# Linear attention and a gated MLP on one core: loads and transposes as a stream of their own, weight fold and norms re-paced, scheduler constants changed

## The chip, the cores and the metric

The kernel runs on one core of a Trainium2 chip. The metric is device time in microseconds (us) of one execution. Repeated executions of one kernel here mostly lie within 0.5% of each other (the six of the kernel before: 284.86 to 285.74 us; the widest fast set of a changed kernel, e11: 284.05 to 286.36); one execution of one experiment, e6, fell into a much slower state (487.29 us at a granted clock of 0.559) and is set aside below. The engines are PE (matrix multiply), DVE (vector), ACT (scalar, with the exponentials), POOL (general purpose) and SP, whose queue issues all DMA transfers of this kernel, one after the other (79 in the trace of the kernel before, no two issues overlapping).

## The reference

One input `x` of 2048 tokens by 640 is normalised, then goes through a linear attention with 32 heads of 20 and through a gated MLP of width 1536. The sum of both and of `x` is the result.

```python
def _A_ref(x, wqkv, w_phi, wo):
    qkv = (x @ wqkv).reshape(B, S, 3, H, Dh) ...            # q, k, v: [1, 32, 2048, 20]
    pq = einsum("bhsd,hdf->bhsf", q, w_phi);  pk = einsum("bhsd,hdf->bhsf", k, w_phi)
    phi_q = concatenate([softmax(pq), softmax(-pq)], -1)    # phi_k the same from pk
    kv = einsum("bhsf,bhsd->bhfd", phi_k, v);  z = einsum("bhsf->bhf", phi_k)
    o = einsum("bhqf,bhfd->bhqd", phi_q, kv) / (einsum("bhqf,bhf->bhq", phi_q, z)[..., None] + 1e-6)
    return o... @ wo
def _B_ref(x, w1, w3, w2):
    return (silu(x @ w1) * (x @ w3)) @ w2
xn = layernorm(x)
return x + _A_ref(xn, ...) + _B_ref(xn, ...)
```

## The kernel before

Tokens are handled in 16 tiles of 128. For each tile: load `x`, layer norm (statistics on DVE, the power on POOL, the application on DVE or ACT), transpose to `xnT` (tiles 0 to 3 on PE, tiles 4 to 15 by a transposing DMA), then keys (`Wkp`) and values (`wv`). `Wkp` is the key weight with `w_phi` folded in; this "fold" is 30 small matmuls that need the transposed `wk` (in `wqkT`) and a block diagonal `BDc` that POOL builds from `w_phi` (`phi_s`). MLP groups (10 matmuls of 512 columns each) do not depend on the attention and serve as filler.

The order of instructions on each engine is fixed when the program is built, by a list scheduler in Python. Each part of the work is a generator, a "stream". The scheduler keeps estimated times, takes the stream whose next piece can start first, and appends it. In the traces PE keeps to that order, waiting on semaphores: the ten matmuls that e9's list has before the keys of tile 4 instead of after those of tile 5 start at 30.67 us in the kernel before, and in e9 they run in the stretch from 22.76 to 26.86, before those keys. So an estimate that is too hopeful costs a real stall: in the hole of 2.0 us shown below, PE stands still although matmuls that could run come later in its list.

```python
    def commit(self, ops):                      # the scheduler's model of a DMA
        ...
            if o.dma:
                self.free[o.eng] = t + 0.45
                if "T" == o.part:
                    self.free[o.eng] = t + max(2.6, o.cost / 150e3)
                self.bus = max(self.bus, t + 0.4) + o.cost / 340e3
                o.end = self.bus + 1.6
...
    def loads():
        x(0, 1); x(1, 2); x(2, 4)                               # [cut: written out]
        P.dma("SP", wv[:], wqkv_t[:, :, 2 * D:3 * D])
        P.dma("SP", phi_s[:], phi_t)
        P.dma("SP", wqkT[:, DC:2 * DC, :], A_wqkv[:, D:2 * D], True)   # transposing
        x(4, 8)
        w13(0, 512)
        x(8, 12)
        w13(512, 1024)
        x(12, 16)
...
    def attention():
        ...
        yield v(2)
        for dc in range(DC):
            yield lambda dc=dc: fold_mm(1, dc, banks(2))
        yield v(3)
        for t in range(T):
            yield lambda t=t: k_tile(t, banks(2))
            done["k"] = t + 1
            if 2 <= t < 14:
                yield from transposed(t + 2)
            if t == 3:
                yield lambda: w13(1024, 1536)
            if t == 5:
                yield lambda: P.dma("SP", wqkT[:, 0:DC, :], A_wqkv[:, 0:D], True)
            if t >= 4:
                yield v(t)
        ...
    streams = [norms(), attention(), k_norms(), o_transposes(), mlps(), outs()]
```

The softmax here doesn't subtract the row's maximum and nothing guards it: scores larger than these inputs give would overflow.

Of the kernel before, what the change touches and what calls it, by code (L numbers as in the profile page):

```python
# [9 lines left out]
D = 640  # L10
# [3 lines left out]
T = S // 128  # L14
DC = D // 128
# [27 lines left out]
class _Program:  # L43
# [3 lines left out]
    def __init__(self, nc):  # L47
        self.nc = nc
        self.eng = {"PE": nc.tensor, "ACT": nc.scalar, "DVE": nc.vector,
                    "POOL": nc.gpsimd, "SP": nc.sync}  # L50
        self.base = {}
        self.ops = []
        self.free = dict.fromkeys(ENGINES, 0.0)
        self.bus = 0.0
        self.last_w = {}
        self.last_r = {}
        self.bank = {}
        self.pending = None
        self.pool = None
# [107 lines left out]
    def commit(self, ops):  # L167
        for o in ops:
            o.idx = len(self.ops)
            o.deps = self.find_deps(o)  # L170
            t = self.free[o.eng]
            for d in o.deps:
                t = max(t, d.end + 0.07)
            o.start = t
            if o.dma:
                self.free[o.eng] = t + 0.45
                if "T" == o.part:
                    self.free[o.eng] = t + max(2.6, o.cost / 150e3)
                self.bus = max(self.bus, t + 0.4) + o.cost / 340e3
                o.end = self.bus + 1.6  # L180
            else:
                o.end = t + o.cost
                self.free[o.eng] = o.end
            self.ops.append(o)
            if o.eng == "POOL" and not o.dma:
                self.pool = o
            for g in o.reads:
                if isinstance(g, tuple):
                    self.bank.setdefault(g, {})[o.eng] = o
                else:  # L190
                    self.last_r.setdefault(g, {})[("dma", o.idx) if o.dma else o.eng] = o
            for g in o.writes:
                if isinstance(g, tuple):
                    self.bank.setdefault(g, {})[o.eng] = o
                else:
                    self.last_w[g] = o
                    self.last_r.pop(g, None)
# [45 lines left out]
def bass_parallel_sum__linear_kernel_hedgehog__glu_gated_swiglu__prompt_kernel(  # L243
# [154 lines left out]
    def w13(a, b):  # L398
        P.dma("SP", w1_s[:, :, a:b], w1_t[:, :, a:b])
        P.dma("SP", w3_s[:, :, a:b], w3_t[:, :, a:b])  # L400

    def loads():
        def x(a, b):
            P.dma("SP", x_tok[:, a:b, :], x_t[:, a:b, :])

        x(0, 1)
        x(1, 2)
        x(2, 4)
        P.dma("SP", wv[:], wqkv_t[:, :, 2 * D:3 * D])
        P.dma("SP", phi_s[:], phi_t)  # L410
        P.dma("SP", wqkT[:, DC:2 * DC, :], A_wqkv[:, D:2 * D], True)
        x(4, 8)
        w13(0, 512)
        x(8, 12)
        w13(512, 1024)
        x(12, 16)


    def consts():
# [45 lines left out]
    def xn_transpose(t, k):  # L465
        for dc in range(DC):
            tr(PSb[:, k * 1024 + 128 * dc:k * 1024 + 128 * dc + 128],
               x_tok[:, t, 128 * dc:128 * dc + 128])
        src = PSb[:, k * 1024:k * 1024 + D].rearrange("p (c n) -> p c n", n=128)
        evac(xnT[:, :, t * 128:(t + 1) * 128], src)  # L470
# [152 lines left out]
                       default=0.0)  # L623
        return min(range(0, 8, n), key=free_at)

    done = dict.fromkeys(("ln", "t", "k", "n", "kv", "q", "o", "h"), 0)

    def norms():
        yield lambda: (loads(), consts())
        for t in range(4):  # L630
            yield lambda t=t: ln_stats(t, 1)
            if t % 2:
                yield lambda t=t: ln_apply(t - 1)
                done["ln"] = t
                yield lambda t=t: ln_apply(t)
                done["ln"] = t + 1
        yield block_diag
        for t in range(4, T, 2):
            while t > done["t"] + 4:
                yield None  # L640
            yield lambda t=t: ln_stats(t, 2)
            if t > 4:
                yield lambda t=t: ln_apply(t - 2)
                yield lambda t=t: ln_apply(t - 1)
                done["ln"] = t
        yield lambda: ln_apply(T - 2)
        yield lambda: ln_apply(T - 1)
        done["ln"] = T
        yield consts_late

    def k_norms():
        for t in range(T):
# [5 lines left out]
    def transposed(t):  # L658
        while done["ln"] <= t:
            yield None  # L660
        if t < 4:
            yield lambda: xn_transpose(t, banks(1))
        else:
            yield lambda: P.dma("SP", xnT[:, :, t * 128:(t + 1) * 128], x_tok[:, t, :], True)
        done["t"] = t + 1

    def attention():
        def v(t):
            return lambda: v_tile(t, banks(2))

        yield lambda: warm_up(10, True)
        yield from transposed(0)
        yield lambda: warm_up(4, False)
        yield from transposed(1)
        yield v(0)
        yield v(1)
        yield from transposed(2)
        yield from transposed(3)
        yield v(2)
        for dc in range(DC):  # L680
            yield lambda dc=dc: fold_mm(1, dc, banks(2))
        yield v(3)
        for t in range(T):
            yield lambda t=t: k_tile(t, banks(2))
            done["k"] = t + 1
            if 2 <= t < 14:
                yield from transposed(t + 2)
            if t == 3:
                yield lambda: w13(1024, 1536)
            if t == 5:  # L690
                yield lambda: P.dma("SP", wqkT[:, 0:DC, :], A_wqkv[:, 0:D], True)
            if t >= 4:
                yield v(t)
            if 9 <= t < 14:
                yield lambda dc=t - 9: fold_mm(0, dc, banks(2))
        yield lambda: P.dma("SP", wo_s[:], A_wo.rearrange("(c p) d -> p c d", p=128))
        for fc in range(DC):
            yield lambda fc=fc: q_proj(0, fc, banks(1))
        while done["n"] < T:
            yield None  # L700
        for fc in range(DC):
            for sg in range(2):
                yield lambda fc=fc, sg=sg: kv_sum(sg, fc, banks(1))
        done["kv"] = 1
        yield lambda: P.dma("SP", w2_s[:], B_w2.rearrange("(c p) d -> p c d", p=128))
        yield lambda: (load_xres(0), load_xres(1))
        for b in range(NB):
            for j in range(4):
                t = 4 * b + j
                yield lambda t=t: q_tok(t, banks(4))  # L710
                done["q"] = t + 1
                if b + 1 < NB:
                    for fc in range((5 * j + 3) // 4, (5 * j + 8) // 4):
                        yield lambda b=b, fc=fc: q_proj(b + 1, fc, banks(1))
# [8 lines left out]
    def mlps():  # L723
        for b in range(NB):
            for fc in range(FC):
                while done["t"] < 4 * b + 4 or b == 2 and done["t"] < T or b == 3 and not done["kv"]:
                    yield None
                yield lambda b=b, fc=fc: mlp(b, fc, banks(2))
            done["h"] = b + 1
# [4 lines left out]
                yield None  # L734
            yield lambda t=t: out_tile(t, banks(2))

    streams = [norms(), attention(), k_norms(), o_transposes(), mlps(), outs()]
    n = len(streams)
    heads, alive = [None] * n, [True] * n
    while any(alive):  # L740
        best = None
        for i in range(n):
            if heads[i] is None and alive[i]:
                s = next(streams[i], StopIteration)
                if s is StopIteration:
                    alive[i] = False
                else:
                    heads[i] = s
            if heads[i] is None:
                continue  # L750
            save = nmlp[0], len(finish)
            ops = P.step(heads[i])
            after = nmlp[0], finish[save[1]:]
            nmlp[0] = save[0]
            del finish[save[1]:]
            if any(o.eng == "PE" for o in ops):
                at = max(P.ready(ops), P.free["PE"] + 0.15)
            else:
                at = P.start_of(ops[0])
                if i == 2:  # L760
                    at -= 4.0
                if i == 0 and at < P.free["PE"] + 2.0:
                    at = -1.0
            if best is None or at < best[0]:
                best = (at, i, ops, after)
        if best is None:
            continue
        at, i, ops, after = best
        nmlp[0] = after[0]
        finish.extend(after[1])  # L770
        P.commit(ops)
        heads[i] = None
# [61 lines left out]
```

## Time and profile before

| | before |
|---|---|
| median of 6 runs | 285.38 us (284.86 to 285.74) |
| span of the profiled run | 283.2 us, granted PE clock 1.000 |
| first useful matmul / end of the last | 6.01 / 280.7 us |

The page of the kernel before; in part 2 each digit is the busy share of one fortieth of the span, in tenths, and part 4 is the chain of waits that ended last:

```profile
span 283.2 us, 4601 instructions
PE 274.6 (97%) x1873; PEld 168.4 (59%) x1890; DVE 181.1 (64%) x317; ACT 107.8 (38%) x194; POOL 59.5 (21%) x90
PE   7897999999999999999999999999999999999996
PE 82%; DVE 6%; DMA 6%; SPq 3%; issue 2%; ACT 0%
```

A slice is 7.08 us. Only the first four slices and the last have visible room; the fourth, from 21.2 to 28.3 us, stands at 7. From the fifth on PE is the limit: busy 90% or more in each slice but the last, and 82% of the chain. Note that 1873 matmuls are recorded but 1890 weight loads: 17 matmul records are missing.

What PE waited for, kernel before (total us, times, longest):

```profile
PE PS L101 <- DMA xnT<-x_tok: 1.8, 1, 1.8
PE PS L101 <- DVE t_68 L101: 1.6, 2, 1.3
PE PS L101 <- DVE x_tok L101: 0.8, 2, 0.6
PE PS L101 <- ACT xnT L101: 0.5, 1, 0.5
```

The longest wait is for one transposed tile. The timeline of PE around it (start, duration, what, count; in brackets the idle time before it and who ended it):

```profile
16.99 5.60 PE L101 MATMUL PS<-Wkp,xnT 128*128 128x320 bf16 x40
22.64 2.10 PE L101 MATMUL PS<-xnT,w_s 128*128 128x512 bf16 x9
26.59 1.53 PE L101 MATMUL PS<-Wkp,xnT 128*128 128x320 bf16 x10 [1.84 <-DMA xnT<-x_tok]
```

Four tiles of keys, one MLP group (one record missing), then nothing until the keys of tile 4 at 26.59. The issues on the SP queue in that stretch, same columns:

```profile
11.62 3.13 SPq L113 DMA_DIRECT2D w_s<-in_B_w_dram  x2
14.79 1.79 SPq L113 DMA_DIRECT2D x_tok<-in_A_x_dram  x1
18.36 4.95 SPq L113 DMA_TRANSPOSE xnT<-x_tok  x2
```

And the same moment in the chain of waits, in order of time: the transpose issued at 18.36 landed 8.18 us later, at 26.54.

```profile
18.36 8.18 DMA xnT<-x_tok
26.54 0.05 issue
26.59 9.12 PE PS L101 x60
```

The three loads ahead of it (w1 and w3 columns 512 to 1024, x tiles 12 to 15, 1.9 MB) landed at 22.3, 24.2 and 26.0 (landing times that no line here shows are read from the landing records of the packed trace). Of the eight later transposes of the same form, issued from 49.05 us on with no load ahead, six landed in 2.6 us, the other two in 3.3 and 3.9.

### The profile page before, as it was taken

What the parts mean: (1) busy time and instruction counts of PE and PEld (TensorE: products, weight loads), DVE (VectorE), ACT (ScalarE), POOL (GpSimd) and SP (SyncE); (2) the same over time, 40 slices, a digit from 0 to 9 for tenths busy, and PEclk for the clock granted to TensorE, in tenths of its full rate; (3) what the DMA queues carried; (4) which work ended last, traced back from release to release, by engine and by line L of the source; (5) the groups of instructions that cost most, each with busy time, mean ns of one, the idle gap of its engine ahead of it and who ended that gap; (6) DMA issues with size and microseconds to landing.
All of it is one profiled execution on the core that took longest, in us unless ns stands there. A gap on an engine that the chain in (4) does not pass through costs nothing.

```text
span 283.2 us, 4601 instructions
## 1 busy us (share of the span) xinstructions
PE 274.6 (97%) x1873; PEld 168.4 (59%) x1890; DVE 181.1 (64%) x317; ACT 107.8 (38%) x194; POOL 59.5 (21%) x90
## 2 busy tenths in 40 slices
PE   7897999999999999999999999999999999999996
PEld 2664644666765965555555555544467777777774
DVE  4589986987772468998998999999731212121212
ACT  2596644697976035446446453332200000000000
POOL 4548970387586100000000000000000000000000
PEclk9999999999999999999999999999999999999999
DMA  7999900242500065411112111132002131312211
GB/s 215 282 352 264 262 1 1 49 46 56 155 0 2 0 203 146 44 29 23 25 23 45 27 24 23 29 44 46 0 2 93 49 93 46 95 54 85 70 51 46
DMA packets 39654, 21.96 MB, mean 78 GB/s; under 512 B 26704, under 2 KB 39632, under 8 KB 39632
## 3 DMA queue, kind: packets, MB, share of 16 engines
q1 hardware_dynamic: 39632, 21.66, 30.6%
q8 instruction: 15, 0.25, 0.4%
q14 instruction: 7, 0.06, 0.1%
HBM read 12.81 MB, written 2.62 MB: 54 GB/s over the span
## 4 chain that ended last, share of the span: by engine, by line
PE 82%; DVE 6%; DMA 6%; SPq 3%; issue 2%; ACT 0%
PE PS L101 82%; SPq L113 3%; DMA xnT<-x_tok 3%; DMA x_tok<-in_A_x_dram 3%; DVE prod L101 2%; DVE t_68 L101 1%; DVE den_s L101 1%; DVE hT_79 L101 1%; DVE g_s L101 0%; DVE hT_71 L101 0%; DVE pr_s L101 0%; DVE xres L101 0%; ACT e_s L101 0%; DVE o_tok L101 0%
## 5 line engine op out<-in xcount | busy, mean ns | idle before, releaser
L101 PE MATMUL PS<-xnT,w_s 128*128 128x512 bf16 x468 | 105.9, 379 | 1.0 <-DVE t_68 L101 0.3
L101 PEld LDWEIGHTS PS<-xnT,w_s 128*128 128x128 bf16 x480 | 46.6, 98 | 55.6 <-DVE prod L101 0.6
L101 DVE TENSOR_TENSOR xres<-PS,xres 128x640 bf16<-128x640 f32 (+2 forms) x17 | 13.4, 786 | 60.0 <-PE PS L101 60.0
L101 ACT ACTIVATE th<-PS 128x512 f32<-128x512 f32 x48 | 28.7, 598 | 53.5 <-PE PS L101 53.5
L101 DVE SCALAR_TENSOR_TENSOR t_68<-th,PS 128x512 bf16<-128x512 f32 x48 | 32.6, 680 | 14.2 <-ACT th L101 14.2
L101 POOL TENSOR_TENSOR ekt<-ekt,rS_62 128x640 bf16<-128x640 bf16 x32 | 39.7, 1270 | 7.3 <-DVE rS_62 L101 7.2
L101 DVE TENSOR_REDUCE S_61<-ekt 128x64 f32<-128x1280 bf16 x16 | 23.5, 1467 | 6.9 <-ACT ekt L101 6.9
L101 PE MATMUL PS<-Wkp,xnT 128*128 128x320 bf16 x160 | 23.9, 299 | 1.8 <-DMA xnT<-x_tok 1.8
L101 PE MATMUL PS<-wv,xnT 128*128 128x320 bf16 x160 | 24.2, 299 | 0.7 <-ACT xnT L101 0.5
L101 PE MATMUL PS<-wo_s,oT 128*128 128x320 bf16 (+2 forms) x160 | 24.5, 299 | 0.0
L101 DVE TENSOR_TENSOR prod<-PS,g_s 128x1280 bf16<-128x1280 f32 x16 | 23.9, 1491 | 0.5
L101 ACT ACTIVATE ekt<-PS 128x640 bf16<-128x640 f32 x32 | 20.6, 706 | 6.8 <-PE PS L101 6.7
L101 PE MATMUL PS<-xnT,Wqp 128*128 128x512 bf16 x95 | 22.6, 379 | 0.3
L101 PEld LDWEIGHTS PS<-Wkp,xnT 128*128 128x128 bf16 x160 | 15.4, 98 | 8.0 <-DMA xnT<-x_tok 2.3
L101 PEld LDWEIGHTS PS<-wv,xnT 128*128 128x128 bf16 x160 | 15.4, 98 | 7.6 <-ACT xnT L101 0.7
L101 PEld LDWEIGHTS PS<-wo_s,oT 128*128 128x128 bf16 x160 | 15.7, 98 | 6.3
L101 DVE BATCH_NORM_STATS2 bst<-x_tok 128x6 f32<-128x320 bf16 x32 | 15.2, 476 | 5.1 <-DMA x_tok<-in_A_x_dram 4.6
L101 PEld LDWEIGHTS PS<-xnT,Wqp 128*128 128x128 bf16 x100 | 9.4, 98 | 8.8
L101 ACT ACTIVATE v_82<-PS 128x640 bf16<-128x640 f32 x16 | 11.5, 716 | 8.3 <-PE PS L101 8.0
L101 ACT ACTIVATE e_s<-PS 128x64 f32<-128x64 f32 x32 | 9.0, 283 | 14.5 <-PE PS L101 13.5
L101 PE MATMUL PS<-w_s,hT_79 128*128 128x320 bf16 (+2 forms) x96 | 13.9, 299 | 0.0
L101 PE MATMUL PS<-w_s,hT_77 128*128 128x320 bf16 x96 | 13.7, 299 | 0.0
(57 smaller groups left out, 268.3 us busy)
## 6 DMA issues: line engine op xcount, KB each, us to landing
w_s<-in_B_w_dram SPq DMA_DIRECT2D x6, 640.0 KB, 7.1
xres<-in_A_x_dram SPq DMA_DIRECT2D x16, 160.0 KB, 2.4
out_dram<-xres SPq DMA_DIRECT2D x15, 160.0 KB, 1.8
x_tok<-in_A_x_dram SPq DMA_DIRECT2D x3, 640.0 KB, 8.4
w_s<-in_B_w_dram SPq DMA_DIRECT2D x1, 1920.0 KB, 8.4
wv<-in_A_wqkv_dram SPq DMA_DIRECT2D x1, 800.0 KB, 5.5
wo_s<-in_A_wo_dram SPq DMA_DIRECT2D x1, 800.0 KB, 4.9
x_tok<-in_A_x_dram SPq DMA_DIRECT2D x2, 160.0 KB, 2.4
```

Of the source, the lines that this page charges most:

```text
L101: o = _Op(eng, lambda: m(*args, **kw), r, w, cost)
L113: o = _Op(eng, lambda: m(out, in_), self.regions(in_), self.regions(out), nbytes, True)
```

## The change

The intent: issue the transposes from a stream of their own and put later weight loads behind them, so that the keys need not wait; fold `wk` whenever it lands; load `phi` and `wv` first, `x` tiles 2 and 3 after them; pace the norms by finished keys; and correct the constants of the scheduler's DMA model. No arithmetic changes. The core of the diff:

```diff
-        self.free = dict.fromkeys(ENGINES, 0.0)
+        self.free = dict.fromkeys(ENGINES, 0.8)
-                    self.free[o.eng] = t + max(2.6, o.cost / 150e3)
-                self.bus = max(self.bus, t + 0.4) + o.cost / 340e3
+                    self.free[o.eng] = t + max(1.3, o.cost / 150e3)
+                self.bus = max(self.bus, t + 0.5) + o.cost / (280e3 if o.part else 320e3)
...
-        x(2, 4)
+        P.dma("SP", phi_s[:], phi_t)
         P.dma("SP", wv[:], wqkv_t[:, :, 2 * D:3 * D])
-        P.dma("SP", phi_s[:], phi_t)
+        load_x(2, 4)
         P.dma("SP", wqkT[:, DC:2 * DC, :], A_wqkv[:, D:2 * D], True)
-        x(4, 8)
+        load_x(4, 8)
         w13(0, 512)
-        x(8, 12)
-        w13(512, 1024)
-        x(12, 16)
+        load_x(8, 12)
...                                             # norms(): block_diag after tile 1, and
-            while t > done["t"] + 4:
+            while t > done["k"] + 6:
                 yield None
...
+    def fold_k():                               # a stream; before: in line after v(2)
+        for dc in range(DC):
+            yield lambda dc=dc: fold_mm(1, dc, banks(2))
+        done["f"] += 1
...
+    def loads():                                # a stream; before: inside attention()
+        while done["t"] < 4: yield None
+        for t in range(4, T):
+            while done["ln"] <= t: yield None
+            yield lambda t=t: P.dma("SP", xnT[:, :, t * 128:(t + 1) * 128], x_tok[:, t, :], True)
+            done["t"] = t + 1
+            if t == 7:
+                yield lambda: (w13(512, 1024), load_x(12, 16))
+                done["w"] = 8
+            if t == 9:
+                yield lambda: w13(1024, 1536)
+                done["w"] = 12
+                yield lambda: P.dma("SP", wqkT[:, 0:DC, :], A_wqkv[:, 0:D], True)
+                done["f"] = 2
...
-    streams = [norms(), attention(), k_norms(), o_transposes(), mlps(), outs()]
+    streams = [norms(), attention(), k_norms(), loads(), fold_k(), o_transposes(), mlps(), outs()]
-                if i == 2:
+                if i == 2 and at < P.free["PE"] + 3.0:
                     at -= 4.0
```

More of the change, by code (lines that the diff above doesn't have):

```diff
@@ L400, in w13, with load_x, first_loads @@
         P.dma("SP", w3_s[:, :, a:b], w3_t[:, :, a:b])
-    def loads():
-        def x(a, b):
-            P.dma("SP", x_tok[:, a:b, :], x_t[:, a:b, :])
-        x(0, 1)
-        x(1, 2)
-        x(2, 4)
+    def load_x(a, b):
+        P.dma("SP", x_tok[:, a:b, :], x_t[:, a:b, :])
+    def first_loads():
+        load_x(0, 1)
+        load_x(1, 2)
+        P.dma("SP", phi_s[:], phi_t)
         P.dma("SP", wv[:], wqkv_t[:, :, 2 * D:3 * D])
-        P.dma("SP", phi_s[:], phi_t)
+        load_x(2, 4)
         P.dma("SP", wqkT[:, DC:2 * DC, :], A_wqkv[:, D:2 * D], True)
-        x(4, 8)
+        load_x(4, 8)
         w13(0, 512)
-        x(8, 12)
-        w13(512, 1024)
-        x(12, 16)
+        load_x(8, 12)
     def consts():
@@ L624, in banks @@
         return min(range(0, 8, n), key=free_at)
-    done = dict.fromkeys(("ln", "t", "k", "n", "kv", "q", "o", "h"), 0)
+    done = dict.fromkeys(("w", "ln", "t", "f", "k", "n", "kv", "q", "o", "h"), 0)
     def norms():
-        yield lambda: (loads(), consts())
+        yield lambda: (first_loads(), consts())
         for t in range(4):
@@ L636, in norms @@
                 done["ln"] = t + 1
-        yield block_diag
-        for t in range(4, T, 2):
-            while t > done["t"] + 4:
+            if t == 1:
+                yield block_diag
+        todo = []
+        for t in range(4, T + 2, 2):
+            if t == T or t > done["k"] + 6:
+                for u in todo:
+                    yield lambda u=u: ln_apply(u)
+                    done["ln"] = u + 1
+                todo = []
+            if t == T:
+                break
+            while t > done["k"] + 6:
                 yield None
             yield lambda t=t: ln_stats(t, 2)
-            if t > 4:
-                yield lambda t=t: ln_apply(t - 2)
-                yield lambda t=t: ln_apply(t - 1)
-                done["ln"] = t
-        yield lambda: ln_apply(T - 2)
-        yield lambda: ln_apply(T - 1)
-        done["ln"] = T
-        yield consts_late
+            for u in todo:
+                yield lambda u=u: ln_apply(u)
+                done["ln"] = u + 1
+            todo = [t, t + 1]
+        yield consts_late
+    def fold_k():
+        for dc in range(DC):
+            yield lambda dc=dc: fold_mm(1, dc, banks(2))
+        done["f"] += 1
+    done["w"] = 4
     def k_norms():
@@ L660, in transposed @@
             yield None
-        if t < 4:
-            yield lambda: xn_transpose(t, banks(1))
-        else:
-            yield lambda: P.dma("SP", xnT[:, :, t * 128:(t + 1) * 128], x_tok[:, t, :], True)
+        yield lambda: xn_transpose(t, banks(1))
         done["t"] = t + 1
+    def loads():
+        while done["t"] < 4:
+            yield None
+        for t in range(4, T):
+            while done["ln"] <= t:
+                yield None
+            yield lambda t=t: P.dma("SP", xnT[:, :, t * 128:(t + 1) * 128], x_tok[:, t, :], True)
[8 more added lines that the diff above has]
+                done["f"] = 2
     def attention():
@@ L679, in attention @@
         yield v(2)
-        for dc in range(DC):
-            yield lambda dc=dc: fold_mm(1, dc, banks(2))
         yield v(3)
+        while done["f"] < 1:
+            yield None
         for t in range(T):
+            while done["t"] <= t:
+                yield None
             yield lambda t=t: k_tile(t, banks(2))
             done["k"] = t + 1
-            if 2 <= t < 14:
-                yield from transposed(t + 2)
-            if t == 3:
-                yield lambda: w13(1024, 1536)
-            if t == 5:
-                yield lambda: P.dma("SP", wqkT[:, 0:DC, :], A_wqkv[:, 0:D], True)
             if t >= 4:
@@ L694, in attention @@
             if 9 <= t < 14:
+                while done["f"] < 2:
+                    yield None
                 yield lambda dc=t - 9: fold_mm(0, dc, banks(2))
@@ L725, in mlps @@
             for fc in range(FC):
-                while done["t"] < 4 * b + 4 or b == 2 and done["t"] < T or b == 3 and not done["kv"]:
+                while done["t"] < 4 * b + 4 or done["w"] <= fc or b == 2 and done["t"] < T or b == 3 and not done["kv"]:
                     yield None
```

## The prediction

> **What bounds the kernel now.** The matrix engine. The page gives PE 97% of a 283.2 us span, and the chain of waits is PE for 82%. The start-to-start pitch in the timeline is 0.216 us for a 512-column matmul, so PE streams back to back[...]. I count pitches, not busy shares. Summing pitches, useful matmuls need about 268 us (264.6 recorded, plus an estimated 3.7 for the roughly 17 records missing). What is left to win:
> - the start, to the first real matmul at 6.01 us, and four warm-up matmuls after it: kept;
> - small holes between 7.5 and 15.6 us: 1.8 us together (the wait views name the norms of tiles 2 and 3 and one xnT copy, 1.1 us);
> - one hole at 24.4 to 26.6 us, 2.0 us: PE <- DMA xnT<-x_tok;
> - about 0.9 us near 187 to 194 us, PE <- DVE (t);
> - the tail after the last matmul, 2.5 us.
> So about 5 us (1.8%) is there at all; over 2% would need more than the holes hold.
>
> **What the change does to them.**
> 1. The 2.0 us hole. The transpose of token tile 4 is issued at 18.36 and lands at 26.54, 8.2 us, because w1, w3 (512 to 1024) and x tiles 12 to 15 (1.9 MB, issued from 11.6 us, landing at 22.3, 24.2 and 26.0) sit ahead of it. Uncrowded transposes of the same form later (49.05 us) land in 2.6 us. The change issues those loads after tile 7's transpose, so tile 4 should land at about 21 to 21.5 us (estimate: 18.4 + 2.6 to 3), before PE finishes the keys of tile 3 at 22.3. The hole goes: -2.0 us.
> 2. The fold of wk can run when wk lands (10.9 us, before: 13.5) and fills PE's waits for tiles 2 and 3. But x tiles 2 and 3 now queue behind wv's 0.8 MB: they land at about 8 us, not 5.3, and their norms slip by about 1 us. Net -0.3 us (between -0.8 and +0.5).
> 3. The later weight loads land about 8 us later. First use of w1, w3 (512 to 1024) needs four MLP groups and several key tiles done first, over 15 us of PE work, so no wait.
> 4. Norms paced by keys move DVE and POOL work earlier, without changing its amount. DVE is 64% busy overall but 92% from 140 to 180 us; a differently mixed order can lose or win up to 1 us there. Expected 0.
> 5. The scheduler's new constants only change order; work and bytes stay the same.
>
> All of it is on the chain, since PE is continuous from 26.6 to 280.7 us: a hole removed early moves the end by as much, unless DVE gives it back after 170 us.
>
> **Prediction.** 285.4 - 2.0 - 0.3 = 283.1 us, range 281.2 to 285.3. Faster by over 2%: 0.03; within 2%: 0.95; slower: 0.02.
>
> **What would show it.** Right: the wait PE <- DMA xnT gone; tile 4's transpose landing about 3 us after issue; key tile 0 starting at 16.5 to 17.3 us; wk's fold before the second pair of transposes; recorded matmul counts and PE's total pitch unchanged. Wrong: PE waiting on w_s, on Wkp or on the x_tok norms of tiles 2 and 3; a larger PE <- DVE t wait after 170 us.
>
> **What would make it wrong.** PE in program order stalls where the scheduler's model is too hopeful: its transposes now cost 1.3 us of issue, the trace shows 1.2 to 3.2 in the crowded stretch. Several such stalls would eat the 2 us.

## The result, and the profile after

| | before | after |
|---|---|---|
| median of 6 runs | 285.38 us | 283.12 us (282.78 to 283.43) |
| ratio after / before | | 0.9921 (95%: 0.9908 to 0.9935) |
| span of the profiled run | 283.2 us | 281.4 us |

Executions over 1.5% slower than the fastest of the same kernel are left out of the means. A ratio is the mean time of one kernel's fast runs over that of the other's in the same rounds, so it is not quite the ratio of the medians quoted. All these runs are at clock 1.0. The gain of 0.8% is clear of noise.

The page of the kernel after:

```profile
span 281.4 us, 4619 instructions
PE 275.2 (98%) x1890; PEld 168.6 (60%) x1890; DVE 180.6 (64%) x317; ACT 108.6 (39%) x194; POOL 59.3 (21%) x90
PE   7799999999999999999999999999999999999996
PE 87%; DVE 6%; DMA 3%; issue 1%; SPq 1%; ACT 1%
```

The fourth slice of PE is now full; the second fell from 8 to 7. All 1890 matmuls are recorded here, so "PE busy" rose by 0.6 us for no reason of work: it is the missing records of before. PE's waits after:

```profile
PE PS L101 <- DVE t_68 L101: 1.6, 2, 1.3
PE PS L101 <- DMA wqkT<-in_A_wqkv_dram: 0.9, 1, 0.9
PE PS L101 <- DMA wv<-in_A_wqkv_dram: 0.5, 1, 0.5
PE PS L101 <- ACT Wkp L101: 0.5, 1, 0.5
```

The wait for the DMA of `xnT` is gone; three small new ones (1.9 us) stand where those for `x_tok` and the copy of `xnT` (1.3 us) stood. The timeline of PE shows both:

```profile
8.13 2.88 PE L101 MATMUL PS<-wv,xnT 128*128 128x320 bf16 x20 [0.49 <-DMA wv<-in_A_wqkv_dram]
11.89 0.47 PE L101 MATMUL PS<-BDc,wqkT 128*128 128x140 bf16 x6 [0.88 <-DMA wqkT<-in_A_wqkv_dram]
...
14.35 2.89 PE L101 MATMUL PS<-wv,xnT 128*128 128x320 bf16 x20 [0.48 <-ACT Wkp L101]
...
17.40 2.32 PE L101 MATMUL PS<-xnT,w_s 128*128 128x512 bf16 x10
19.55 6.96 PE L101 MATMUL PS<-Wkp,xnT 128*128 128x320 bf16 x50
```

The fold (the 128x140 matmuls) now fills in around tiles 2 and 3, an MLP group stands before the keys, and the keys of tiles 0 to 4 run unbroken. The SP queue after, in the same stretch:

```profile
19.40 5.17 SPq L113 DMA_TRANSPOSE xnT<-x_tok  x4
24.62 1.15 SPq L113 DMA_DIRECT2D w_s<-in_B_w_dram  x2
25.81 0.53 SPq L113 DMA_DIRECT2D x_tok<-in_A_x_dram  x1
```

The four transposes go first, each landing 2.6 to 2.7 us after its issue (tile 4 at 22.01), the loads after them.

### A sum that closes

Busy shares cannot account for 2 us here, so I used start-to-start intervals of PE. For each kind of matmul the median interval is its pitch (0.216 us at 512 columns, 0.136 at 320). What an interval exceeds its pitch by, if over 0.05 us, is a hole; warm-up matmuls (the kernel's `warm_up`) are left out. The pitches sum to 268.6 us in every fast trace with all records. Where records are missing (all of them of 512 columns) the sum falls short, and each missing one looks like a hole of one pitch, so this is taken off. Before: 8.54 - 17 x 0.216 = 4.87 us of holes. After: 3.26 us.

| profiled run | loads of w1, w3, x 12-15 | constants | span | holes | span less holes |
|---|---|---|---|---|---|
| before | early | old | 283.2 | 4.87 | 278.3 |
| after | late | new | 281.4 | 3.26 | 278.1 |
| e1_late_loads | late | old | 281.2 | 2.98 | 278.2 |
| e9_before_new_model | early | new | 281.3 | 3.05 | 278.3 |
| e2_early_loads | early | new | 281.8 | 3.58 | 278.2 |
| e8_early_loads_old_model | early | old | 283.9 | 5.83 | 278.1 |
| e7_old_model | late | old | 280.8 | 2.51 | 278.3 |
| e3_fold_inline | late | new | 282.7 | 4.54 | 278.2 |
| e4_old_first_loads | late | new | 282.7 | 4.46 | 278.2 |
| e5_x_before_wv | late | new | 281.2 | 2.95 | 278.3 |
| e10_split_wv | late | new | 283.2 | 5.09 | 278.1 |
| e11_split_wv_wk | late | new | 283.0 | 4.70 | 278.3 |

The last column is constant to 0.3 us over twelve kernels. So nearly every difference of span here is a difference of PE holes, and the question is only which holes a version has. One fast trace is not in the table: after_again, a second profile of the kernel after, has 2.70 us of holes and 278.6 us without them. There the first transposes and the warm-up matmuls after them, up to 7.3 us, ran at twice the usual pitch (the four warm-up matmuls took 1.45 us, against 1.03 in the first profile), which this count mostly does not see as a hole; so single traces can differ by 0.5 us in this column. Two of the runs below are built on the kernel before (e1, e9), the others on the kernel after.

### The profile page after: what moved, and what is told of

Its sections match the earlier page's. It is cut to its first block, busy times and chain, and to the rows that moved or that the text cites. A ratio compares the mean times of both kernels' runs of the same rounds, so it can differ in the third digit from the quotient of the medians.

```text
span 281.4 us, 4619 instructions
## 1 busy us (share of the span) xinstructions
PE 275.2 (98%) x1890; PEld 168.6 (60%) x1890; DVE 180.6 (64%) x317; ACT 108.6 (39%) x194; POOL 59.3 (21%) x90
## 4 chain that ended last, share of the span: by engine, by line
PE 87%; DVE 6%; DMA 3%; issue 1%; SPq 1%; ACT 1%
PE PS L101 87%; DMA wqkT<-in_A_wqkv_dram 3%; DVE prod L101 2%; DVE t_68 L101 1%; SPq L113 1%; DVE den_s L101 1%; DVE hT_71 L101 1%; ACT Wkp L101 0%; DVE g_s L101 0%; DVE hT_79 L101 0%; DVE pr_s L101 0%; ACT xnT L101 0%; DVE xres L101 0%; ACT e_s L101 0%; DVE o_tok L101 0%
## 5 line engine op out<-in xcount | busy, mean ns | idle before, releaser
L101 PE MATMUL PS<-xnT,w_s 128*128 128x512 bf16 x480 | 107.2, 379 | 0.3 <-DVE t_68 L101 0.3
L101 PE MATMUL PS<-xnT,Wqp 128*128 128x512 bf16 x100 | 23.7, 379 | 0.0
L101 PE MATMUL PS<-w_s,hT_71 128*128 128x320 bf16 x96 | 13.7, 299 | 0.0
L101 PE MATMUL PS<-w_s,hT_76 128*128 128x320 bf16 x96 | 13.7, 299 | 0.0
```

The source lines that it names most:

```text
L101: o = _Op(eng, lambda: m(*args, **kw), r, w, cost)
```

## The experiments

Theory A, of the prediction: the 2 us hole is a transpose queued behind the early loads; issuing the loads later closes it. Rival B: the new pacing of norms, or the scheduler's constants, carry the gain. From the first results came theory C: what matters as much is whether the schedule has placed work over the late landing.

### e1: late loads alone, on the kernel before

```diff
         x(8, 12)
-        w13(512, 1024)
-        x(12, 16)
...
             if t == 5:
+                yield lambda: (w13(512, 1024), [x tiles 12 to 15])
+                done["w"], done["x"] = 8, 1
+                yield lambda: w13(1024, 1536)      # was at t == 3
```
(The norms of tiles 12 to 15 and the MLP groups from 4 on wait for `done["x"]` and `done["w"]` in the schedule.)

> The kernel before with one part of the change: w1, w3 (512 to 1024) and x tiles 12 to 15 are issued after the transpose of tile 7 (MLP groups and norms that need them wait for that point in the schedule). Nothing else is changed. Theory A (the 2 us hole is a transpose queued behind these loads): the transpose of tile 4 lands about 3 us after its issue at 18.4 us, the PE wait on xnT is under 0.3 us, time 283.2 to 283.6 us, ratio to before about 0.993. Rival B (the gain is of the new pacing of norms, or of the scheduler's constants): the time stays within 0.5 us of before, 285 us or more.

Measured: 283.33 us median (282.93 to 284.52), ratio 0.9938 (0.9904 to 0.9973). The transpose of tile 4, issued at 18.30, landed at 20.90. No PE wait on the DMA of `xnT` is left, and the keys of five tiles run unbroken. This part of the change alone is sufficient for about 1.9 us; rival B is not needed for it. PE's timeline in e1 from 20 us on (the first line is cut by the window):

```profile
19.76 4.24 PE L101 MATMUL PS<-Wkp,xnT 128*128 128x320 bf16 x30
23.83 2.32 PE L101 MATMUL PS<-xnT,w_s 128*128 128x512 bf16 x10
```

### e2: the loads early again, on the kernel after

```diff
         load_x(8, 12)
+        w13(512, 1024)
+        load_x(12, 16)
...
-                yield lambda: (w13(512, 1024), load_x(12, 16))
```

> The kernel after with the same loads back in the first burst, ahead of the transposes; all else as after. Theory A: the transposes of tiles 4 and on land at 26 us or later, PE gets a wait on xnT of 1 to 3 us back, time 284.8 to 286 us. Rival B: the time stays near 283.1 us.

Measured: 283.70 us (283.61 to 284.22), ratio 0.9943. Theory A's number missed. The transpose did land late, at 27.00 (issued 19.45), but PE lost only 0.1 us there:

```profile
24.86 2.32 PE L101 MATMUL PS<-xnT,w_s 128*128 128x512 bf16 x10
27.13 1.52 PE L101 MATMUL PS<-Wkp,xnT 128*128 128x320 bf16 x10
```

The scheduler, with its new constants, expected the late landing and put an MLP group in front of the keys of tile 4. Late loads are sufficient, then, but not necessary. This gave theory C, tested by the next two.

### e9: the new constants alone, on the kernel before

```diff
-        self.free = dict.fromkeys(ENGINES, 0.0)
+        self.free = dict.fromkeys(ENGINES, 0.8)
-                    self.free[o.eng] = t + max(2.6, o.cost / 150e3)
-                self.bus = max(self.bus, t + 0.4) + o.cost / 340e3
+                    self.free[o.eng] = t + max(1.3, o.cost / 150e3)
+                self.bus = max(self.bus, t + 0.5) + o.cost / (280e3 if o.part else 320e3)
```

A comparison of the two programs shows what this did: on PE, one MLP group (10 matmuls) moved from after the keys of tile 5 to before the keys of tile 4. The SP and POOL lists are identical, and DVE and ACT only follow.

> The kernel before with only the scheduler's four constants of the change. By program order this moves one thing: one MLP group (10 matmuls, 2.16 us) from after tile 5's keys to just before tile 4's keys; the order of loads and transposes is the same. Theory C (the hole is as much a matter of not having placed work over a transpose that lands late as of the late landing; the new constants place it): the transpose of tile 4 still lands at about 26.5 us, but the PE wait on xnT falls from 1.8 us to under 0.3 us and the time to 283.2 to 283.8 us. Theory A alone (only the order of loads closes the hole): 285 us, the wait stays.

Measured: 283.47 us (282.80 to 284.03), ratio 0.9936 (0.9920 to 0.9953). The transfers stayed where they were, to within 0.4 us: tile 4's transpose was issued at 18.41 and landed at 26.22 (before: 18.36 and 26.54). But PE was busy meanwhile with two groups (19 of 20 matmuls recorded):

```profile
22.76 4.26 PE L101 MATMUL PS<-xnT,w_s 128*128 128x512 bf16 x19
26.86 1.52 PE L101 MATMUL PS<-Wkp,xnT 128*128 128x320 bf16 x10
```

Moving ten matmuls, with every transfer where it was, is worth about as much as e1. Theory C's number held, theory A alone is out.

### e8: loads early and the old constants, on the kernel after

The edit is e2's and the reverse of e9's.

> The kernel after with the loads early again and also the scheduler's old constants. In program order PE then has the keys of tiles 0 to 4 in one run, without the MLP group that stood between tiles 3 and 4 with the new constants. Theory C: the hole returns, PE waits on xnT 1.5 to 2.5 us, time 284.9 to 286 us, against 283.7 us with the new constants. Rival (the fold as a stream and the pacing carry the gain): under 284 us.

Measured: 285.60 us (285.31 to 287.31), ratio 1.0029 (1.0006 to 1.0052). Theory C held. Everything else of the change is still in this kernel, and its gain is gone. That includes the new pacing of the norms and the changed condition for `k_norms` in the last lines of the diff, neither of which was tested alone. The hole is back (the window cuts the first line):

```profile
19.82 5.46 PE L101 MATMUL PS<-Wkp,xnT 128*128 128x320 bf16 x39
27.45 1.52 PE L101 MATMUL PS<-Wkp,xnT 128*128 128x320 bf16 x10 [2.17 <-ACT ekt L101]
```

Read this line with care. It names ACT, not the DMA. The instruction waits on two semaphores, ACT's and that of tile 4's transpose, and the trace has the latter landing at 27.32. The profile names whichever event came last before the start, and ACT was in an unbroken run of exponentials whose latest ended at 27.39. In the kernel after the same keys started at 24.99, with ACT at the same place in its run. So I take the DMA to be the cause; that ACT had released the bank long before is argued from this comparison, not shown.

### e7 and after_again: the fourth corner

e7 is the kernel after with the old constants only (the reverse of e9's edit); after_again is the kernel after, unchanged, on the same chip.

> The kernel after with only the scheduler's old constants; loads late, as after. It is the fourth corner of loads (early, late) by constants (old, new). Theory D (late loads and new constants take away one and the same hole, so either alone suffices and the two do not add): within 0.5 us of after, 282.7 to 283.6 us, no PE wait on xnT over 0.5 us before 30 us. Rival (each is worth 1 to 2 us of its own): 284.2 us or more.

> The kernel after, unchanged, to stand beside the other runs of this call on the same chip. Theory: 283.1 us, ratio to before about 0.992.

Measured: e7 282.87 us (282.56 to 283.20), ratio 0.9911; after_again 283.19 us (283.02 to 283.55), ratio 0.9923. Theory D held: the two corrections do not add. Medians (on different chips; the kernel before had 285.21 to 285.47):

| | old constants | new constants |
|---|---|---|
| loads early, rest as before | 285.32 (before) | 283.47 (e9) |
| loads late, rest as before | 283.33 (e1) | not run |
| loads early, rest as after | 285.60 (e8) | 283.70 (e2) |
| loads late, rest as after | 282.87 (e7) | 283.19 (after_again) |

Either correction is worth 1.9 to 2.7 us where the other is missing. Where it is present, late loads add 0.5 us (e2 against after_again, with overlapping intervals) and the new constants nothing (e7 is 0.3 us faster without them). There is one hole, and it can be closed by having the data earlier or the filler in place.

### e3: the fold in line again, on the kernel after

```diff
         yield v(2)
+        for dc in range(DC):
+            yield lambda dc=dc: fold_mm(1, dc, banks(2))
         yield v(3)
-        while done["f"] < 1:
-            yield None
...
-    streams = [norms(), attention(), k_norms(), loads(), fold_k(), o_transposes(), mlps(), outs()]
+    streams = [norms(), attention(), k_norms(), loads(), o_transposes(), mlps(), outs()]
```

> The kernel after with the fold of wk back at its old place in line (after v of tile 2), not a stream of its own; load order as after. Theory (the fold as a stream is worth little or nothing, since PE then waits 0.9 us for wk and 0.5 us for a Wkp copy while both x tiles and wk land late): within 0.5 us of after, 282.7 to 283.6 us. Rival (the stream is worth a good part of the gain): 0.7 us or more slower than after, 283.8 us or more.

Measured: 284.55 us (283.94 to 285.74), ratio 0.9974 (0.9942 to 1.0007). My theory missed and the rival held: within this change the stream is worth about 1.4 us (1.3 us by the holes of the traces). The trace splits it. Holes before 20 us are 2.64 us against 2.35 (PE waits 1.5 us for the late norms of tiles 2 and 3, with no fold to fill in), and a new hole of 1.0 us stands at tile 8:

```profile
32.63 1.52 PE L101 MATMUL PS<-wv,xnT 128*128 128x320 bf16 x10
34.97 1.26 PE L101 MATMUL PS<-Wkp,xnT 128*128 128x320 bf16 x8 [0.82 <-DMA xnT<-x_tok]
```

Tile 8's transpose was issued at 30.93, behind x tiles 12 to 15 (landed 33.80), and landed at 34.93. It is the first hole again, four tiles later: PE reached keys before their transpose landed, with no filler between. In the kernel after an MLP group sits at 35.85 and PE comes to tile 8 at 38.01.

### e4, e5, e6: the order of the first loads

```diff
 after: x0, x1, phi, wv, x2-3       e4: x0, x1, x2-3, wv, phi (as before)
                                    e5: x0, x1, phi, x2-3, wv
                                    e6: e5 and the fold in line (e3's edit)
```

> The kernel after with the first loads in their old order (x tiles 2 and 3, then wv, then phi); fold still a stream. Theory (x early helps, phi late makes no difference as long as it lands before wk at 11 us, though the block diagonal on POOL, 2.05 us, then starts at 8 us and pushes the norms of tiles 2 and 3): near the run with phi third and x before wv, 282.6 to 283.4 us. Rival (phi first is what the new order is for): 283.6 us or more.

> The kernel after with x tiles 2 and 3 loaded before wv again, phi still third; fold still a stream. Theory (moving x tiles 2 and 3 behind wv cost about 1 us by delaying their norms): tiles 2 and 3 land about 5.5 us, their transposes and values can fill the wait for wk, PE's holes before 16 us fall from 2.3 us to about 1.3 us or less, time 282.0 to 282.8 us. Rival (wv later costs as much as x earlier gains): within 0.3 us of after.

> The kernel after with phi third, x tiles 2 and 3 before wv, and the fold of wk in line again. Theory (the fold stream is only needed to cover the late x tiles that the same change made; with x early it is worth under 0.5 us): 282.5 to 283.4 us. Rival (the stream is worth 1 us or more in itself): 283.8 us or more.

Measured: e4 284.17 us (283.80 to 284.99), ratio 0.9964; e5 282.84 us (282.60 to 283.05), ratio 0.9910 (0.9879 to 0.9941); e6 284.43 us, the median of its five fast runs (283.77 to 285.23), ratio 0.9975.

e5, with five runs, decides nothing: 282.84 us lies just above its theory's range and also within 0.3 us of the kernel after, as its rival has it. It has 1.69 us of holes before 20 us, not the 1.3 expected. The wait for `wk` fell from 0.9 us to none, but the one for `wv` stayed at 0.5 (it landed at 8.16). e4 missed its theory by 0.8 us: with phi behind wv (landed at 8.53) the block diagonal starts on POOL at 8.59 us, not at 6.58 as in e5, and the power for the norms of tiles 2 and 3, which comes after it in POOL's list, at 10.53, not at 8.60 (POOL appears among PE's waits, with 0.3 us). In the kernel before, the block diagonal came after those norms. Holes before 20 us are 3.0 us, and 0.5 us more at tile 8 as in e3. So phi early is worth something here, more than I thought. e6 missed too: the fold in line costs about 1.6 us against e5 even with x early. Where it loses stays open, since e6's profile fell into a slow execution (487.29 us, granted clock 0.559: 0.66 in the first 20 us, 0.56 in every later stretch), which I do not compare; no run shows its cause.

### e10, e11: splitting loads, to beat both

```diff
+ e10: e5's order, and wv as two loads: row blocks 0-2, then 3-4
+ e11: as e10, and the transposing load of wk as five, one per column block of the fold
```

> The kernel after with phi third, x tiles 2 and 3 before wv, and the load of wv in two parts (three and two of its five row blocks), so that the values of tile 0 can start on the first part. Theory: the first part lands about 0.9 us before the second, the PE wait on wv (0.5 us) goes, 282.2 to 282.7 us. Rival (the start is bound by the copy of xnT or the second part): as without the split, 282.8 us.

> As the run with wv in two parts, and the transposing load of wk in five parts, one for each column block of the fold. Theory: the fold can start when its first part has landed, before 11 us, so the PE wait on wk is gone: 282.0 to 282.6 us. Rival (five issues on the queue cost more than one, x tiles 4 to 7 land later, and the gain is given back): 283 us or more.

Measured: e10 284.51 us (283.99 to 284.96), ratio 0.9964; e11 284.91 us (284.05 to 286.36), ratio 0.9987. Both theories missed. The intended waits shrank: the one for `wv` from 0.5 us in e5 to 0.3 in e10, the one for `wk` from 1.0 us in e10 to nothing in e11. But in e10 that wait for `wk` was itself new (none in e5; `wk` landed at 11.68, not at 11.10), and PE met another transfer too early. e10, waits of PE:

```profile
PE PS L101 <- DMA wqkT<-in_A_wqkv_dram: 2.7, 2, 1.7
PE PS L101 <- DMA wv<-in_A_wqkv_dram: 0.3, 1, 0.3
```

The second of the `wqkT` waits, 1.7 us, is the fold of the query weight at 45.21, whose load landed at 45.08. In e11, where the rival's reason held (the queue came to x tiles 4 to 7 at 10.64 us, against 9.08 in e5), w1 and w3 (columns 0 to 512) landed at 17.00 and 20.03, not at 15.71 and 17.58 as in e5, and the first MLP group waited for both:

```profile
17.35 1.02 PE L101 MATMUL PS<-xnT,w_s 128*128 128x512 bf16 x4 [1.75 <-DMA w_s<-in_B_w_dram]
20.08 1.25 PE L101 MATMUL PS<-xnT,w_s 128*128 128x512 bf16 x5 [1.70 <-DMA w_s<-in_B_w_dram]
```

About 3.4 us given back (one record of this group is missing, so up to 0.2 less) for 1.4 us won: the transposes, values and fold that come before this group were done at 15.43 us, against 16.79 in e5. No version clearly beat the kernel after. e7 and e5 are 0.3 us lower in the median; e7's interval against before overlaps that of after_again, and e5 was not run beside the kernel after.

## Why the prediction was right, and where it was not

The number held: 283.1 predicted, 283.12 measured. The steps held less well than the sum, and the agreement to 0.02 us is luck: the start came out 0.8 us worse than predicted in the trace, and small terms that the prediction did not have made up for it (sum below).

- **The bound: right.** PE's pitches were put at about 268 us; complete traces have 268.6. The pitch of 0.216 us at 512 columns is the median in the traces of before and after, and no interval is under 0.215; one matmul is recorded as 0.379 us long, so within a group the records of neighbours overlap, with no gap. "About 5 us of holes" was 4.87 us.
- **Step 1, the hole of 2.0 us: right in size, incomplete in cause.** The tile 4 transpose landed 2.6 us after its issue, as estimated, and the wait is gone. It was issued 1.0 us later than before, so it landed at 22.0, not at 21 to 21.5. That late loads suffice is shown by e1 and e7. That they are the only thing in the change to close the hole, as the prediction has it, is refuted by e9 and e2.
- **Step 2, the fold and the first loads, -0.3 us: wrong in sign.** Holes before 20 us went from 1.82 us (as defined above) to 2.35 us, +0.5 us, the very edge of the stated -0.8 to +0.5. x tiles 2 and 3 landed at 8.92 (5.35 before), wk at 11.76 (10.89 before), and PE waited for wk, for wv and for a copy of Wkp. But single traces scatter as much. The first transposes, values and fold, the same work in both orders, were done at 16.99 to 17.11 us in the three traces with the old order of first loads (before, e1, e9), and at 16.72 to 17.52 in the five with the new one and the fold as a stream (after 17.39, after_again 17.18, e2, e7, e8); `wk` landed at 10.83 to 10.89 in the former and at 11.09 to 11.89 in the latter. What stands is that the expected gain did not come. The wait on Wkp (0.5 us) is one that the prediction had listed as a sign of being wrong. Nor did the prediction see that, with the new order, the fold as a stream is worth 1.4 us (e3) in avoiding worse.
- **The keys' start: missed.** Key tile 0 began at 19.55, not at 16.5 to 17.3, because an MLP group of 2.15 us was placed before it. This costs nothing; it is work moved. Without it the keys would have begun at 17.40.
- **Step 3, no wait on w1 and w3 (512 to 1024): right.** They landed at 29.1 and 31.0 us, and the fifth MLP group, the first to need them, came at 71.0. (The wait in e11 is for the columns 0 to 512.)
- **Step 4, nothing won or lost at DVE late: right.** 0.9 us of holes between 179 and 194 us in both traces.
- **Step 5, "the scheduler's new constants only change order": true, and the wrong thing to conclude from it.** It was counted as zero. Alone they are worth 1.85 us (e9), because order is what decides whether PE sits in front of a late transfer. They added nothing here only because step 1 had taken the same hole.

In the traces: -2.0 for the hole, +0.5 at the start, -0.15 for a first matmul at 5.86 rather than 6.01 us, -0.14 for a small hole at 70.5 us of the kernel before that the kernel after does not have, together -1.8, as the spans differ. The medians of timed runs differ by 2.26. The rest is which executions were profiled: that of the kernel before took 284.90 us, 0.5 under its median, that of the kernel after 283.25, 0.1 above.

## What to carry to other kernels

In this statically ordered program a late transfer cost nothing once enough independent work stood in front of its consumer (e9: tile 4's transpose landed at 26.22 us, and PE came to its keys at 26.86), so look at what PE does in the gap before making the transfer faster: moving ten matmuls did here what re-ordering 1.9 MB of loads did. Fixes for one hole did not add here (e7 282.87 us with one of them, after_again 283.19 with both), so test each alone and both together before giving either credit. And when the schedule comes from a model, any edit, even one that removes a wait, can march the busiest engine into another late transfer sooner (0.8 us at tile 8 in e3, 1.7 us at the fold of the query weight in e10); read the waits again after each edit.

## What else the traces show

- Bulk loads issued early delayed a later small transfer that was needed sooner. With 1.9 MB ahead, tile 4's transpose took 8.2 us from issue to landing (before); with those loads moved behind it, 2.6 us (e1: issued 18.30, landed 20.90). In the traces of before and after all 79 transfers landed in the order of their issue; in the stretch of the hole at 22.3, 24.2, 26.0 and 26.5 us. No run shows why.
- The transposing load of the 640 by 640 key weight held the issuing queue for 5.6 us before and 6.4 us after, against 0.5 us for the plain load of the equally large wv. A 128-token transpose held it for 1.2 to 1.3 us in 11 of the 12 of the kernel after (2.4 us in the other), and tile 4's for 3.2 us in the kernel before, behind the loads.
